# Hash attention and MLP on one core: the first two chunks run by another table of the same operations

## The chip, the cores and the metric

The kernel runs on one core of a Trainium2 chip. The metric is the device time of one execution in microseconds (us). TensorE (PE; its weight loads are shown as PEld), VectorE (DVE), ScalarE (ACT), GpSimd (POOL) and SyncE (SP) each work through a list of instructions of their own, in order, and wait for one another by semaphores.

## The reference

What is computed, cut to what matters (q, k, v are 4 batches x 8 heads x 768 tokens x 64; d_model is 512, the hidden width 2048):

```python
    q_bits = (np.einsum('bhsd,dk->bhsk', q, proj) > 0).astype(np.int64)
    k_bits = (np.einsum('bhsd,dk->bhsk', k, proj) > 0).astype(np.int64)
...
    mask = q_bucket[:, :, :, None] == k_bucket[:, :, None, :]
    scores = scale * np.matmul(q, k.transpose(0, 1, 3, 2))
    scores = np.where(mask, scores, -1000000000.0)
    scores = scores - np.max(scores, axis=-1, keepdims=True)
    attn = np.exp(scores)
    attn = attn / (np.sum(attn, axis=-1, keepdims=True) + 1e-09)
    return np.matmul(attn, v).astype(np.float32)
...
    xn = (x - mu) / np.sqrt(var + 1e-06) * g_ln
    ch = np.maximum(xn @ w_ch1, 0.0) @ w_ch2
    return (x + ch).astype(np.float32)
```

## The kernel before

**Chunks, pairs, groups.** The work is cut into 12 chunks: 4 batches x 3 stretches of 256 query tokens. A chunk's attention has 4 pairs of heads with 3 groups each, 12 units. A unit has a scores half (L513: four matmuls of 256 columns into the PSUM tile sc, then one exponential on ScalarE, L519, into ex) and a values half (L534: 16 or fewer small matmuls av <- ex, vaug). The third group of a pair ends with a quotient on VectorE (L562, L572). In batch 0 an epsilon term is added on TensorE before it (L549): with six matmuls if the pair's values have not been summed yet, with one if they have. A chunk's MLP is a norm on VectorE, eight "ups" (hp, L653) and eight "downs" (o, L675). In chunk n the attention of chunk n is interleaved with downs of chunk n-2 and ups of chunk n-1.

**Operands.** Scores are taken with 70 rows: 64 of q or k in bf16 and 6 of hash bits, side by side in the tile slots. For batch 0 each head's q and k are transposed on TensorE (tpose, L237), evacuated from PSUM to qkT (L247, L249 on VectorE, L251 on ScalarE), cast into slots in two halves, par 0 and par 1 (L196 on VectorE or GpSimd, L192 on ScalarE), hashed on TensorE (L356 for one head, L384 for a pair), compared with zero on VectorE (bits, L365, L391), and the bit rows are copied into slots (L196, L192). For the batches after it GpSimd narrows q and k (N, L270), a transposing DMA on SP's queue writes slots (L294), the odd tokens are copied to their place (L194 by DMA, or L196 on GpSimd), and the bits go through DRAM (L326, L333). The xnT of all chunks but the first is a transposing DMA on SP's queue too (L637). SP's queue also has all loads of q, k, v (L147, L182) and all outputs (L684). GpSimd issues the loads of the weights (L699, L706).

**What sets the order.** The first two chunks, half of chunk 2 and the preparation of batches 0 and 1 are written out by hand in a string, FIRST_TWO, that the function first_two runs from left to right; each engine gets its instructions in that order. The letters, with the head or half first and the engine that is to do it (V, A, G) last: T is a transpose with its evacuation (T31V: head 3, k, evacuated by VectorE; a small s or a at the end puts it into a buffer of the score or the values pool of PSUM instead of the common pool mm), C a cast (C40G: head 4, par 0, GpSimd), h and H a hash of a head or a pair, r and B bit rows, P the values of a pair, R their sums, z and Z matmuls that only keep TensorE busy, W weights, S, X, Y, U, M parts of the MLP of chunks 0 and 1, L, N, V, K, O, D the preparation of batch 1, Q squares for a check at the end. "<" is the next scores half and ">" the next values half of a list of units that the string ORDER gives. In the texts S2.1 is the scores half of unit 1 of chunk 2, V0.11 the values half of unit 11 of chunk 0. In chunks 2 to 8 a dictionary, plan, names what is prepared for the batches after: three parts of a chunk (parted by "|"), each spread over fillers.

**Buffers.** sc has 2 buffers, and transposes marked s take turns in them; av has 2, with those marked a and z; mm has 2; ex has 3; qkT has 4.

Of the kernel before, what the change touches and what calls it, by code (L numbers as in the profile page):

```python
# [28 lines left out]
def kernel(  # L29
# [753 lines left out]
    FIRST = 6  # L783
    mlp = {n: mlp_steps(*chunks[n], xs[n]) for n in range(2)}

    ORDER = "020 000 0012 0212 01 10 20 30 11 31 21 12"
    FIRST_TWO = """
z3 Z20 p T00V T01Aa C00A C01G T10As h0m T11Aa r0VVGA C10V h1m C11V < z3 r1VVVV T20A T30As < T31V T21V < P0 C30V e C31G C20V >
< >
H1 P1 >  # L790
T40As B1VVVV < T41A W0 < >
R1V < R0V C41V >
T50Aa C40G C21A T51V >
< C50V H2 < >
T60Va T61A < C51G T70V >
T71V < P3 B2VGAV >
>
C60G < C61G H3 >
< P2 C71V B3VVVV W1 >
< S0 L0 R2V b < >  # L800
R3V v0 C70G < W2 >
< >
< >
Z12 < >
< >
< S1 >
X0 N00 >
X1 < Y0A K011 < Y1V L1 >
V0 < N01 >
U0 U1 < U2 >  # L810
K001 O0 K000 >
< U3 < U4 >
< K010 U5 >
K101 D0 U6 < >
>
< U7 < Q010 Q011 K110 M >
K100 K111 >
Q001 Q000
"""

    def first_two():
# [94 lines left out]

        groups = [[int(c) for c in g] for g in ORDER.split()]
        seq = [(n, 3 * j + g) for j, n, *gs in groups for g in gs or range(3)]
# [7 lines left out]
                run(op)  # L926

    plan = {
# [264 lines left out]
```

## Time and profile before

| | us |
|---|---|
| median of 3 runs | 304.8 (304.37 to 306.12) |
| the profiled execution | 305.38 |
| its span in the trace | 303.7 |

The granted TensorE clock was full (1.00) in the profiled execution. Busy times are of the span. The start of an exponential depends on its scores, the start of values on their exponential. Times are from the span's start. A row of a timeline is start, duration, engine, line, operation, output <- input, and in brackets how long the engine was idle before and what released it; rows that follow one another are merged with a count (x3). In the view by stretches the columns are length, then busy time (with count) of PE, PEld, DVE, ACT and POOL, the granted clock, the share of the DMA engines, and GB/s. In the grouped view a row ends with busy time, mean ns of one, and idle time before with its releaser.

### The profile page before, as it was taken

The numbers are of one execution on the slowest core, as the hardware profiler recorded it, in microseconds if no ns is written. First come the engines' busy times: TensorE is split into PE (matmuls) and PEld (weight loads), VectorE is DVE, ScalarE is ACT, GpSimd is POOL, SyncE is SP. The second block draws the span as 40 slices with busy tenths as digits, with TensorE's granted clock in tenths as the row PEclk, the third lists the DMA queues.
The fourth block names the chain that finished last, engine by engine and source line by source line (L and its number), as shares of the span: only waits on it lengthen the run. The fifth ranks groups of instructions, "written<-read, shape, count | busy, mean of one in ns | idle before, by whom it ended". The sixth has DMA issues, their size and how long they took to land.

```text
span 303.7 us, 7929 instructions
## 1 busy us (share of the span) xinstructions
PE 295.2 (97%) x3285; PEld 224.7 (74%) x3309; DVE 179.8 (59%) x409; ACT 215.6 (71%) x273; POOL 91.3 (30%) x117
## 2 busy tenths in 40 slices
PE   8999899999999999999999999999999999999995
PEld 5677788578688688678678678679679678687564
DVE  1998678845659459634964954633733734646322
ACT  4899986967788778669578687879677667665020
POOL 3559490685403424500831730200300200201100
PEclk9999999999999999999999999999999999999999
DMA  6999999588296379777487274330110210200302
GB/s 197 367 311 252 260 256 185 120 192 260 42 141 194 89 214 200 161 231 246 140 142 205 19 154 113 21 96 2 35 71 2 64 42 2 69 37 3 106 3 73
DMA packets 64361, 40.40 MB, mean 133 GB/s; under 512 B 44864, under 2 KB 60224, under 8 KB 64320
## 3 DMA queue, kind: packets, MB, share of 16 engines
q1 hardware_dynamic: 61024, 35.64, 47.2%
q0 software_dynamic: 3216, 4.20, 7.8%
q8 instruction: 27, 0.44, 0.6%
q14 instruction: 14, 0.11, 0.1%
q10 hardware_dynamic: 80, 0.00, 0.0%
HBM read 27.97 MB, written 6.88 MB: 115 GB/s over the span
## 4 chain that ended last, share of the span: by engine, by line
PE 93%; DVE 2%; ACT 2%; DMA 1%; issue 1%; SPq 0%; DVEq 0%; ACTq 0%
PE hp L653 28%; PE o L675 27%; PE sc L513 20%; PE av L534 11%; PE hash L313 3%; PE tpose L237 2%; ACT ex L519 1%; DMA knat<-in_k_dram 1%; PE av L549 1%; DVE slots L196 1%; PE hash L384 1%; DVE xn L600 0%; DVE bits L365 0%; PE hash L356 0%; ACT slots L192 0%
## 5 line engine op out<-in xcount | busy, mean ns | idle before, releaser
L519 ACT ACTIVATE ex<-sc,expb 128x1024 bf16<-128x1024 f32 x144 | 159.0, 1114 | 55.5 <-PE sc L513 54.0
L653 PE MATMUL hp<-xnT,w_sb 128*128 128x256 bf16 x768 | 97.7, 272 | 0.1
L675 PE MATMUL o<-w_sb,hbuf 128*128 128x512 bf16 (+1 forms) x376 | 93.1, 370 | 1.0
L513 PE MATMUL sc<-slots 70*128 70x256 bf16 x576 | 87.0, 272 | 0.8 <-ACT ex L519 0.4
L653 PEld LDWEIGHTS <-w_sb 128*128 128x128 bf16 x768 | 72.4, 97 | 9.4 <-issue 0.5
L534 PEld LDWEIGHTS <-ex 128*128 128x128 bf16 x1152 | 53.4, 97 | 15.5 <-ACT ex L519 2.3
L513 PEld LDWEIGHTS <-slots 70*128 70x128 bf16 x576 | 52.0, 97 | 15.5 <-issue 2.7
L534 PE MATMUL av<-vaug,ex 128*128 128x65 bf16 x1152 | 58.0, 193 | 0.7 <-ACT ex L519 0.7
L132 DVE TENSOR_SCALAR hbuf<-hp 128x512 bf16<-128x512 f32 x47 | 32.4, 690 | 43.2 <-PE hp L653 42.5
L675 PEld LDWEIGHTS <-hbuf 128*128 128x128 bf16 x400 | 36.9, 97 | 26.6
L136 ACT ACTIVATE hbuf<-hp 128x512 bf16<-128x512 f32 x49 | 29.1, 595 | 17.8 <-PE hp L653 17.3
L680 DVE SCALAR_TENSOR_TENSOR x<-o,rs,x 128x512 f32<-128x512 f32 (+1 forms) x25 | 18.1, 725 | 31.9 <-PE o L675 31.7
L642 POOL TENSOR_SCALAR rs<-mv 128x2 f32<-128x2 f32 x11 | 7.1, 643 | 90.3 <-DVE mv L627 90.3
L419 POOL CAST vaug<-vnat 128x1536 bf16<-128x1536 f32 x6 | 8.8, 1465 | 45.6 <-DMA vnat<-in_v_dram 28.2
L564 DVE TENSOR_SCALAR rc<-av 128x4 f32<-128x4 f32 x36 | 5.7, 157 | 27.9 <-PE av L534 27.9
L572 DVE TENSOR_TENSOR x<-x,rc 128x256 f32<-128x256 f32 x36 | 17.6, 489 | 1.0
L628 DVE SCALAR_TENSOR_TENSOR xn<-x,mv,gbc 128x512 bf16<-128x512 f32 x22 | 17.7, 840 | 0.1
L565 DVE TENSOR_TENSOR x<-av,vsum 128x256 f32<-128x256 f32 x36 | 14.9, 415 | 0.0
L626 DVE BATCH_NORM_STATS2 stats<-x 128x6 f32<-128x512 f32 x22 | 14.1, 677 | 0.2
L218 ACT ACTIVATE qnat<-qnat 128x768 f32<-128x768 f32 x16 | 13.4, 839 | 0.0
L218 ACT ACTIVATE knat<-knat 128x768 f32<-128x768 f32 x16 | 13.4, 836 | 0.0
L428 POOL TENSOR_TENSOR vsum<-vsum,vaug 128x256 f32<-128x256 f32 x18 | 12.7, 708 | 1.1
(87 smaller groups left out, 208.8 us busy)
## 6 DMA issues: line engine op xcount, KB each, us to landing
out_dram<-x SPq DMA_DIRECT2D x23, 256.0 KB
vnat<-in_v_dram SPq DMA_DIRECT2D x7, 768.0 KB
qnat<-in_q_dram SPq DMA_DIRECT2D x11, 384.0 KB
knat<-in_k_dram SPq DMA_DIRECT2D x11, 384.0 KB
w_sb<-in_moe_w_ch_dram POOLq DMA_DIRECT2D x3, 1024.0 KB, 19.1
qnat<-in_q_dram SPq DMA_DIRECT2D x2, 768.0 KB
knat<-in_k_dram SPq DMA_DIRECT2D x2, 768.0 KB
slots<-slots SPq DMA_DIRECT2D x4, 384.0 KB
```

What stands on the lines that cost most here:

```text
L132: nc.vector.tensor_scalar_max(dst, src, 0.0)
L136: nc.scalar.activation(dst, src, AF.Relu if relu else AF.Copy)
L218: done = nc.scalar.activation(src, src, AF.Square, accum_out=sq[:, a, col : col + 1])
L513: nc.tensor.matmul(sc[:, i, :], sl[0:K1, h, 1, kj * P : (kj + 1) * P], sl[0:K1, h, 0, q0 : q0 + CT],)
L519: nc.scalar.activation(ex, sc, AF.Exp, bias=expb[:, 1:2] if b else expb[:, 0:1], scale=scale if b else scale / Q_SCALE,)
L534: nc.tensor.matmul(av[:, h - ha, qi, :], state[g][:, i, qi * P : (qi + 1) * P], va[:, h, CMAP[b][kj], :], start=((g, i, qi) == (0, 0, 0)), ...
L565: nc.vector.tensor_tensor(xv, num, vs[:, ha : ha + 2, :].unsqueeze(2).to_broadcast([P, 2, TT, D]), op=AOP.add,)
L572: nc.vector.tensor_tensor(xv, num, rc.unsqueeze(3).to_broadcast([P, 2, TT, D]), op=AOP.mult)
L628: nc.vector.scalar_tensor_tensor(xn[:, :, i, :], x[:, i, :].rearrange("p (o d) -> p o d", d=P), mv[:, i, 0:1], gbc.rearrange("p (o d) -> p ...
L653: nc.tensor.matmul(hp[:, i, :], w1_sb[:, dt, nt * P : (nt + 1) * P], st["xnT"][:, dt, :], start=(dt == 0), stop=(dt == ND - 1),)
L675: nc.tensor.matmul(o2, st["h"][:, nt, i * P : (i + 1) * P], w2_sb[:, nt, cols], start=(nt == 0), stop=(nt == NH - 1),)
L680: nc.vector.scalar_tensor_tensor(x[:, i, cols], o2, st["rs"][:, i : i + 1], x[:, i, cols], op0=AOP.mult, op1=AOP.add,)
```

## The change

Both strings are replaced by others that hold the same steps, and plan has other entries for chunks 2 and 3. Cut to what says something:

```diff
-    ORDER = "020 000 0012 0212 01 10 20 30 11 31 21 12"
+    ORDER = "000 020 0012 0212 01 10 20 30 11 31 21 12"
...
-z3 Z20 p T00V T01Aa C00A C01G T10As h0m T11Aa r0VVGA C10V h1m C11V < z3 r1VVVV T20A T30As < T31V T21V < P0 C30V e C31G C20V >
+p Z20 T00As z3 T01A T10Va h0m e C01A C00G T11Aa r0VVGA h1m < C10V P0 T20Va C11V < r1VVGV z3 T30A P1 >
...
     plan = {
-        2: "| H11 E10 W11 o10 V11 L20 | J10 N11 T11 o11 N20",
-        3: "J11 E11 T20 W20 O20 | |",
+        2: "| H11 L20 E10 W11 o10 | N11 T11 N20 O11 V11 J10 J11",
+        3: "W20 E11 | T20 | O20",
```

By ORDER the first group of chunk 0 is scored before the first of chunk 2. Of the 16 evacuations VectorE now does 8 (7 before) and ScalarE 8 (9); of the 16 casts VectorE does 6 (7), ScalarE 1 (2), GpSimd 9 (7); of head 1's bit rows GpSimd does one, and of pair 2's two (one before).

ScalarE from the first exponential on, before. ex, sc, qkT and tpose carry numbers here; qkT_237, 243, 325 and 405 are heads 2, 3, 4 and 5:

```order
L519 ACTIVATE ex_227<-sc_222,expb_67 128x1024
L251 ACTIVATE qkT_237<-tpose_238 128x384
L251 ACTIVATE qkT_243<-tpose_244 128x384
L519 ACTIVATE ex_254<-sc_249,expb_67 128x1024
L519 ACTIVATE ex_271<-sc_266,expb_67 128x1024
L519 ACTIVATE ex_292<-sc_287,expb_67 128x1024
L251 ACTIVATE qkT_325<-tpose_326 128x384
L519 ACTIVATE ex_340<-sc_335,expb_67 128x1024
L251 ACTIVATE qkT_325<-tpose_342 128x384
L519 ACTIVATE ex_354<-sc_349,expb_67 128x1024
L519 ACTIVATE ex_386<-sc_381,expb_67 128x1024
L251 ACTIVATE qkT_405<-tpose_406 128x384
```

The same place now (qkT_252, 338 and 376 are heads 3, 4 and 5):

```order
L519 ACTIVATE ex_226<-sc_221,expb_67 128x1024
L519 ACTIVATE ex_242<-sc_237,expb_67 128x1024
L251 ACTIVATE qkT_252<-tpose_253 128x384
L251 ACTIVATE qkT_252<-tpose_273 128x384
L519 ACTIVATE ex_283<-sc_278,expb_67 128x1024
L519 ACTIVATE ex_290<-sc_285,expb_67 128x1024
L519 ACTIVATE ex_328<-sc_323,expb_67 128x1024
L519 ACTIVATE ex_365<-sc_360,expb_67 128x1024
L251 ACTIVATE qkT_338<-tpose_371 128x384
L519 ACTIVATE ex_387<-sc_382,expb_67 128x1024
L251 ACTIVATE qkT_376<-tpose_408 128x384
L519 ACTIVATE ex_430<-sc_425,expb_67 128x1024
```

Two exponentials now stand side by side at the start, and four (S0.1, S0.2, S2.1, S2.2) follow the evacuations of head 3 with nothing between them, where the evacuations of head 4 stood before.

GpSimd from its first cast to the second part of the weights, before:

```order
L196 CAST slots_86<-qkT 64x2x384
L196 COPY slots_86<-bits 6x2x192
L415 CAST vaug_88<-vnat 128x12x64
L196 CAST slots_86<-qkT 64x2x384
L415 CAST vaug_88<-vnat 128x12x64
L699 DMA w_sb<-in_moe_w_ch_dram 128x4x1024 x2
L196 CAST slots_86<-qkT 64x2x384 x2
L415 CAST vaug_88<-vnat_138 128x12x64
L196 COPY slots_86<-bits 6x768
L196 CAST slots_86<-qkT 64x2x384 x2
L415 CAST vaug_88<-vnat_138 128x12x64
```

The same place now, up to the last cast but one:

```order
L415 CAST vaug_88<-vnat 128x12x64
L196 COPY slots_86<-bits 6x2x192
L415 CAST vaug_88<-vnat 128x12x64
L196 CAST slots_86<-qkT 64x2x384 x2
L699 DMA w_sb<-in_moe_w_ch_dram 128x4x1024 x2
L196 CAST slots_86<-qkT 64x2x384
L415 CAST vaug_88<-vnat_138 128x12x64
L196 CAST slots_86<-qkT 64x2x384
L415 CAST vaug_88<-vnat_138 128x12x64
L196 CAST slots_86<-qkT 64x2x384 x3
L196 COPY slots_86<-bits 6x768 x2
```

Behind the first part of the weights stand five casts, two copies of bit rows and the values of two pairs (vaug <- vnat_138) in a row, and one more cast follows.

SP's queue in chunk 2, before (slots_87 is batch 1's, bits_1184 those of its second half):

```order
L333 DMA slots_87<-bits_d 6x48x32 x3
L684 DMA out_dram<-x 128x512
L326 DMA bits_d<-bits_1184 128x384
L333 DMA slots_87<-bits_d 6x48x32
L294 DMA_TRANSPOSE slots_87<-nat_1287 128x24x128
L684 DMA out_dram<-x 128x512
L147 DMA qnat<-in_q_dram 128x2x384
L147 DMA knat<-in_k_dram 128x2x384
L147 DMA qnat<-in_q_dram 128x2x384
L147 DMA knat<-in_k_dram 128x2x384
L637 DMA_TRANSPOSE xnT<-xn 128x8x128
L333 DMA slots_87<-bits_d 6x48x32 x4
```

And now (bits_1179 are the second half's):

```order
L326 DMA bits_d<-bits_1179 128x384
L147 DMA qnat<-in_q_dram 128x2x384
L147 DMA knat<-in_k_dram 128x2x384
L147 DMA qnat<-in_q_dram 128x2x384
L147 DMA knat<-in_k_dram 128x2x384
L684 DMA out_dram<-x 128x512
L294 DMA_TRANSPOSE slots_87<-nat_1251 128x24x128
L333 DMA slots_87<-bits_d 6x48x32
L194 DMA slots_87<-slots_87 64x24x128
L333 DMA slots_87<-bits_d 6x48x32 x5
L637 DMA_TRANSPOSE xnT<-xn 128x8x128
```

The loads of batch 2 stand ahead of the transposing DMA; the odd tokens (L194) and all bit rows of the second half stand between it and the transposing DMA of the norm.

More of the change, by code (lines that the diff above doesn't have):

```diff
@@ L784 @@
     mlp = {n: mlp_steps(*chunks[n], xs[n]) for n in range(2)}
-    ORDER = "020 000 0012 0212 01 10 20 30 11 31 21 12"
+    ORDER = "000 020 0012 0212 01 10 20 30 11 31 21 12"
     FIRST_TWO = """
-z3 Z20 p T00V T01Aa C00A C01G T10As h0m T11Aa r0VVGA C10V h1m C11V < z3 r1VVVV T20A T30As < T31V T21V < P0 C30V e C31G C20V >
-< >
[L790 to L796, printed above, removed]
->
[L798 to L801, printed above, removed]
-< >
[L803 to L818, printed above, removed]
+p Z20 T00As z3 T01A T10Va h0m e C01A C00G T11Aa r0VVGA h1m < C10V P0 T20Va C11V < r1VVGV z3 T30A P1 >
+T21Vs T31Aa < < H1 C30G >
+>
+< R0V T40Vs C20G >
+W0 C31G < B1VVVV T41A T50Va < R1V P3 C41V C40G >
+T51A >
+< H2 P2 C21G < T60As C50G >
+C51G T61V B2VGAG >
+T70V < T71V C60V >
+< C71V < H3 >
+L0 C61G < W1 b >
+>
+< < B3VVVV W2 C70V >
+S0 R2V < R3V v0 >
+< >
+< Z12 >
+< K011 >
+>
+S1 < >
+X0 X1 < N00 >
+< V0 L1 Y0A >
+< Y1V N01 < >
+U0 U1 Q001 K001 >
+U2 U3 K000 < >
+U4 < K010 K101 < U5 O0 >
+< D0 U6 >
+< >
+< U7 M >
+K110 >
+< Q000 K100 Q011 >
+K111 Q010
 """
```

## The prediction

> **What bounds the kernel now.** The page first: its busy shares and the chain that ended last.
>
> ```profile
> PE 295.2 (97%) x3285; PEld 224.7 (74%) x3309; DVE 179.8 (59%) x409; ACT 215.6 (71%) x273; POOL 91.3 (30%) x117
> ...
> PE 93%; DVE 2%; ACT 2%; DMA 1%; issue 1%; SPq 0%; DVEq 0%; ACTq 0%
> ```
>
> TensorE is busy 97% of the span and makes up 93% of the chain: an average over the whole program, so the next view is the one by stretches of time.
>
> ```profile
> 10.00:20.00 10.00, 9.68 (x132) 8.18 (x133) 9.60 (x22) 9.06 (x13) 4.46 (x5) 1.00 1.06 366
> 20.00:30.00 10.00, 9.50 (x147) 7.08 (x146) 9.20 (x20) 9.54 (x11) 8.65 (x15) 1.00 1.11 252
> 30.00:40.00 10.00, 9.04 (x138) 7.42 (x136) 7.17 (x21) 9.59 (x11) 5.58 (x8) 1.00 1.13 262
> 40.00:50.00 10.00, 10.00 (x135) 8.63 (x133) 6.53 (x11) 7.05 (x9) 5.38 (x7) 1.00 1.23 222
> ```
>
> From 40 us on TensorE is full (10.00 of 10) and the other engines have room: there an edit off TensorE costs or gains nothing unless it makes TensorE wait. From 10 to 40 us TensorE is not full, ScalarE is busy 9.06 to 9.59 of 10, and VectorE 9.60 and 9.20 in the first two rows. That is the part that the table rewrites. So the question is by how much the first MLP matmul (U0 of the table) moves; whatever it moves is kept by the full TensorE behind it.
>
> The chain of waits shows how that point is reached:
>
> ```profile
> 16.72 0.68 PE av L549 x6
> ...
> 19.98 0.11 PE av L549
> ...
> 34.34 0.44 PE sc L513 x4
> 34.78 0.24 PE av L534 x8
> 35.03 0.13 PE av L549
> ...
> 39.90 1.76 PE hp L653 x16
> ```
>
> The last values group of chunk 0 ends at 35.03, then VectorE's norm follows, and the first MLP matmuls run from 39.90. Just ahead of it 0.44 us of scores of chunk 1 stand on the chain.
>
> **Part 1, ScalarE's work in the first stretch.** Two groups of ScalarE between 9.3 and 26.7 us, then rows of its timeline:
>
> ```profile
> L519 ACT ACTIVATE ex<-sc,expb 128x1024 bf16<-128x1024 f32 x11 | 12.1, 1114 | 1.5 <-PE sc L513 1.4
> L251 ACT ACTIVATE qkT<-tpose 128x384 f32<-128x384 f32 x6 | 2.8, 487 | 0.5 <-PE tpose L237 0.4
> ```
>
> ```profile
> 9.38 1.11 ACT L519 ACTIVATE ex<-sc,expb 128x1024 bf16<-128x1024 f32 x1 [0.84 <-PE sc L513]
> 10.58 0.87 ACT L251 ACTIVATE qkT<-tpose 128x384 f32<-128x384 f32 x2
> 11.34 3.21 ACT L519 ACTIVATE ex<-sc,expb 128x1024 bf16<-128x1024 f32 x3
> 14.96 0.49 ACT L251 ACTIVATE qkT<-tpose 128x384 f32<-128x384 f32 x1 [0.40 <-PE tpose L237]
> ...
> 18.27 1.11 ACT L519 ACTIVATE ex<-sc,expb 128x1024 bf16<-128x1024 f32 x1 [0.37 <-PE sc L513]
> ...
> 19.96 0.84 ACT L192 ACTIVATE slots<-qkT 64x768 bf16<-64x768 f32 x1
> 20.83 2.26 ACT L519 ACTIVATE ex<-sc,expb 128x1024 bf16<-128x1024 f32 x2
> ...
> 26.72 2.12 ACT L519 ACTIVATE ex<-sc,expb 128x1024 bf16<-128x1024 f32 x2
> ```
>
> Taken from start to start, an exponential holds ScalarE for 1.07 us (three in 3.21), an evacuation for 0.38 (two from 10.58 to 11.34), a cast for 0.87 (19.96 to 20.83). From the first exponential, 9.38, to the one at 26.72, from which they run on with hardly a pause, are 17.34 us: 11 x 1.07 + 6 x 0.38 + 2 x 0.87 = 15.8, and 1.55 of idle. After the change the same 11 exponentials stand ahead of that point, with five evacuations (heads 3, 3, 4, 5, 6) and one copy: 14.55. **Work saved: 1.25 us** (one evacuation, the cast C21). The first exponential doesn't come earlier: head 0 takes the same steps, with its evacuation and casts only swapped between engines.
>
> **Part 2, the pauses that the new order has.** These are my estimates; the first pause is filled by work that was there before.
>
> ```profile
> 8.68 0.60 PE L513 MATMUL sc<-slots 70*128 70x256 bf16 x4
> ```
>
> From a group's first score matmul to its exponential go 0.70 us (8.68 to 9.38). Scores have two PSUM buffers, and transposes marked s take a turn in them. Before, the evacuations of heads 2 and 3 filled the wait of the second exponential. Now: (a) two exponentials follow at once, then two evacuations, until 9.38 + 2 x 1.07 + 2 x 0.38 = 12.28; the next needs the rows of head 1, which VectorE finishes after two casts, an evacuation and three copies: 11.7 to 12.5, so a pause of 0 to 0.7, I take 0.4. (b) The exponential of S2.1 stands behind hash pair H1 on TensorE: 0.4. (c) T40 takes the buffer between S2.1 and S2.2, so that both use the same one: S2.2's matmuls can start only when the exponential of S2.1 has ended, and ScalarE has nothing between: 0.70 + 0.2 = 0.9. (d) S1.2 stands behind H2, which waits for T51: 0.5. Together 2.2, against 1.55 now: **+0.65**; bounds 0 (every pause covered) to 3.2 (each half as long again).
>
> The values of the first pair now come after its rows are summed, so that six epsilon matmuls (0.68 us) become one (0.11): 0.57 us less on TensorE, in a stretch where ScalarE's pauses decide. I count nothing and keep 0.57 as the lower bound.
>
> **Part 3, GpSimd and VectorE.** GpSimd gets two casts more and two bit-row copies more. VectorE loses a cast, a row copy of each size, and gains an evacuation.
>
> ```profile
> 8.44 0.82 POOL L415 CAST vaug<-vnat 128x768 bf16<-128x768 f32 x1
> 8.52 1.15 DVE L196 CAST slots<-qkT 64x768 bf16<-64x768 f32 x1
> ...
> 10.23 0.56 DVE L196 CAST slots<-qkT 64x768 bf16<-64x768 f32 x1
> ...
> 12.64 0.82 POOL L196 CAST slots<-qkT 64x768 bf16<-64x768 f32 x1 [3.38 <-DVE qkT L249]
> 13.53 1.04 POOL L415 CAST vaug<-vnat 128x768 bf16<-128x768 f32 x1
> 12.98 2.00 DVE L196 CAST slots<-qkT 64x768 bf16<-64x768 f32 x2
> 22.79 0.82 POOL L196 COPY slots<-bits 6x768 bf16<-6x768 bf16 x1 [0.38 <-DVE bits L391]
> ...
> 23.68 1.69 POOL L196 CAST slots<-qkT 64x768 bf16<-64x768 f32 x2
> ...
> 24.21 0.56 DVE L249 COPY qkT<-tpose 128x384 f32<-128x384 f32 x1
> ...
> 30.50 0.82 POOL L196 CAST slots<-qkT 64x768 bf16<-64x768 f32 x1
> ```
>
> VectorE's cast takes 0.56 us alone and 1.15 when GpSimd's cast runs from 8.44 to 9.26: it ends 0.41 after it. The two casts at 12.98 end at 14.98, 0.41 after GpSimd's cast that ends at 14.57. So a cast of VectorE waits out the GpSimd operation that it meets. Four more of 0.8 us are at most 3.3 us of waiting on VectorE. Its evacuations from PSUM are not held: the one at 24.21 takes 0.56 us under two casts of GpSimd. [...]
>
> Where it counts: the bit rows of pair 3 and the second cast of head 7. Before, GpSimd ends that cast at 31.32, and the scores of heads 6 and 7 start about then. Now VectorE does it last. With ScalarE 0.6 us ahead there (1.25 - 0.65), VectorE's chain (pair 3's hash, one quotient, four rows, the cast) ends at about 31.2, and **0.4** of the lead is lost.
>
> **Part 4, the end of the stretch.** V0.11 is moved ahead of S1.4, so that the 0.44 us of scores at 34.34 no longer stand ahead of the last values: **-0.35** on the chain into the norm. The stream transpose that now stands on VectorE before it fits in the wait for those values.
>
> **Part 5, chunks 2 and 3.** The loads of batch 2 are now issued ahead of the transposing DMA of batch 1's second half; the copy of odd tokens goes from GpSimd (2.74 us) to SP's queue.
>
> ```profile
> 64.06 3.68 SPq L294 DMA_TRANSPOSE slots<-nat  x1
> 67.84 0.52 SPq L684 DMA_DIRECT2D out_dram<-x  x1
> 78.82 1.25 SPq L637 DMA_TRANSPOSE xnT<-xn  x1
> 80.18 3.01 SPq L333 DMA_DIRECT2D slots<-bits_d  x4
> 89.83 0.72 SPq L194 DMA_DIRECT2D slots<-slots  x1
> 69.67 2.74 POOL L196 COPY slots<-slots 64x3072 bf16<-64x3072 bf16 x1 [1.83 <-DMA slots<-nat]
> 84.62 1.04 PE L653 MATMUL hp<-xnT,w_sb 128*128 128x256 bf16 x8
> ```
>
> On SP the transposing DMA comes behind the output at 67.84: it is issued by 72.0, lands 1.93 us later (67.74 to 69.67 before), then follow the odd tokens (0.72) and five bit issues (0.75 each): SP is free at 78.5, and the transposing DMA of the norm was issued at 78.82. It feeds the matmuls at 84.62; with 1.25 + 1.93 us of its own it may start as late as 81.4. Cost nothing, with 2.6 us of cover.
>
> **The sum.** -1.25 + 0.65 + 0.4 - 0.35 = -0.55 us. The profiled execution took 305.4 us (span 303.7); its changed form would take 304.8. The median of the runs is 304.8, 0.6 below, so I predict 304.3.
>
> **The rivals.** (A) Faster: the pauses are no longer than before and VectorE keeps up. Then -1.25 - 0.35 - 0.57 = -2.2 us: 302.6. For it speaks that ScalarE is the fullest engine from 20 to 40 us; against it that the new order has a place (c) where nothing can fill ScalarE. (B) Slower: **the GpSimd casts hold VectorE.** Place: VectorE from 19 to 31 us, where GpSimd now does nine operations in a row. Price: 3.3 us of waiting less 0.6 of work taken off VectorE is 2.7 on the cast of head 7; less the 0.35 of part 4 it gives +2.3: 307.1. It decides from the point where that cast ends later than about 31.3. For it: the rows of 1.15 and 2.00; against: half of VectorE's operations there read PSUM. (C) Slower: **SP's queue.** If the transposing DMA behind 1.5 MB of loads lands later than 76.9 instead of 74.0, the norm's transpose is late and TensorE waits at 84.62; five us of lateness cost 2: 306.8 with the rest cancelled. Against: 2.6 us of cover.
>
> **How the numbers follow.** A measurement tells about 0.5%, 1.5 us, from no change here. Forecast (within 1.5 us) 0.55; A 0.17; B 0.16; C 0.12. Faster by over 0.5% is A, 0.17; slower is B and C, 0.28. The range goes from A to B, 302.6 to 307.1; the likeliest case alone is 303.3 to 305.8.
>
> **What would show it.** In the profile after: the first exponential still at 9.4; ScalarE idle for about 0.9 us before the sixth exponential (S2.2); the unbroken run of exponentials from about 26.1 instead of 26.72; the first MLP matmul at 39.2 instead of 39.76; no TensorE wait at 80 to 86. I am wrong if TensorE's stretches after 40 us are no longer full, if VectorE's casts in 19 to 31 us take over 1.2 us each, or if the MLP starts later than 40 us.

## The result and the profile after

The changed kernel takes 306.44 us (median of 12 runs, 304.94 to 309.07), the kernel before 305.03 beside it (12 runs, 304.02 to 306.18). The ratio is 1.0052, with an interval from 1.003 to 1.0074: slower by 1.4 us where 0.5 less than before was forecast. Single executions reach 309, those of before stay under 306.2. Here and below, medians are over all executions, while the ratio and its interval leave out those that are over 1.5% above the fastest of their kernel and follow the means more than the medians, so the ratio is not the quotient of the two medians. The profiled execution of the changed kernel is one of its quickest (305.21 us, span 303.6); that of the kernel before (305.38) stood above its median. So the two traces show where time goes, and not how much it is at the median.

The page of the changed kernel, busy shares and the chain that ended last:

```profile
PE 294.9 (97%) x3280; PEld 223.8 (74%) x3304; DVE 176.2 (58%) x407; ACT 214.6 (71%) x271; POOL 91.6 (30%) x120
...
PE 83%; DMA 6%; POOL 4%; DVE 3%; ACT 2%; issue 1%; SPq 0%; DVEq 0%; POOLq 0%; ACTq 0%
```

TensorE has fallen from 93% to 83% of the chain, and DMA has risen from 1% to 6%: transfers now end waits that lie on the path. ScalarE's timeline of the changed kernel shows the first stretch:

```profile
9.36 2.12 ACT L519 ACTIVATE ex<-sc,expb 128x1024 bf16<-128x1024 f32 x2 [0.84 <-PE sc L513]
11.37 0.87 ACT L251 ACTIVATE qkT<-tpose 128x384 f32<-128x384 f32 x2
12.18 2.12 ACT L519 ACTIVATE ex<-sc,expb 128x1024 bf16<-128x1024 f32 x2
14.87 1.11 ACT L519 ACTIVATE ex<-sc,expb 128x1024 bf16<-128x1024 f32 x1 [0.57 <-PE sc L513]
16.73 1.12 ACT L519 ACTIVATE ex<-sc,expb 128x1024 bf16<-128x1024 f32 x1 [0.74 <-PE sc L513]
...
21.18 1.11 ACT L519 ACTIVATE ex<-sc,expb 128x1024 bf16<-128x1024 f32 x1 [0.35 <-PE sc L513]
```

The first exponential comes at 9.36 as before, and the pauses are 0 (no bracket at 12.18), 0.57, 0.74 and 0.35. TensorE's timeline has the start of the MLP, and behind it two rows that the kernel before doesn't have:

```profile
38.62 1.91 PE L653 MATMUL hp<-xnT,w_sb 128*128 128x256 bf16 x16
...
78.72 0.39 PE L513 MATMUL sc<-slots 70*128 70x256 bf16 x2 [0.37 <-DMA slots<-bits_d]
...
84.50 1.05 PE L653 MATMUL hp<-xnT,w_sb 128*128 128x256 bf16 x8 [0.32 <-DMA xnT<-xn]
```

The MLP starts 1.14 us earlier (38.62 against 39.76), but the matmuls that stood at 84.62 before now stand at 84.50. Most of the lead is lost between 70 and 90 us. The view by stretches of the changed kernel agrees (TensorE's 10 us there were 9.89 and 10.00 full before):

```profile
70.00:80.00 10.00, 9.52 (x95) 6.54 (x96) 7.31 (x15) 7.89 (x11) 4.47 (x4) 1.00 0.51 108
80.00:90.00 10.00, 9.68 (x111) 7.50 (x108) 3.81 (x8) 7.19 (x11) 1.91 (x2) 1.00 0.99 183
```

SyncE's timeline of the changed kernel tells what is late; start and duration are those of the issue:

```profile
61.25 0.43 SPq L147 DMA_DIRECT2D qnat<-in_q_dram  x1
...
62.76 0.47 SPq L147 DMA_DIRECT2D knat<-in_k_dram  x1
64.19 0.36 SPq L684 DMA_DIRECT2D out_dram<-x  x1
64.65 6.12 SPq L294 DMA_TRANSPOSE slots<-nat  x1
70.82 0.74 SPq L333 DMA_DIRECT2D slots<-bits_d  x1
74.38 0.70 SPq L194 DMA_DIRECT2D slots<-slots  x1
75.14 6.07 SPq L333 DMA_DIRECT2D slots<-bits_d  x5
81.31 1.28 SPq L637 DMA_TRANSPOSE xnT<-xn  x1
```

The four loads of batch 2 (two of their rows are left out) stand ahead of the transposing DMA. Its issue takes 6.12 us instead of 3.68, and it lands at 74.37 (in the chain, "64.65 9.72 DMA slots<-nat") instead of 69.67. The odd tokens (74.38) wait for it, and the bits of head 3 are issued behind them, at 75.14; in the kernel before they went ahead of the transposing DMA:

```profile
63.22 0.74 SPq L333 DMA_DIRECT2D slots<-bits_d  x1
```

The other four of the five bit issues, those of the second half, wait once more, until the odd tokens have landed. SyncE's waits between 60 and 90 us name it:

```profile
SPq L333 <- DMA slots<-slots: 2.2, 1, 2.2
```

So the norm's transpose is issued at 81.31 instead of 78.82.

### The profile page after: what moved, and what is told of

Its sections match the earlier page's. It is cut to its first block, busy times and chain, and to the rows that moved or that the text cites. A ratio compares the mean times of both kernels' runs of the same rounds, so it can differ in the third digit from the quotient of the medians.

```text
span 303.6 us, 7917 instructions
## 1 busy us (share of the span) xinstructions
PE 294.9 (97%) x3280; PEld 223.8 (74%) x3304; DVE 176.2 (58%) x407; ACT 214.6 (71%) x271; POOL 91.6 (30%) x120
## 4 chain that ended last, share of the span: by engine, by line
PE 83%; DMA 6%; POOL 4%; DVE 3%; ACT 2%; issue 1%; SPq 0%; DVEq 0%; POOLq 0%; ACTq 0%
PE hp L653 25%; PE o L675 23%; PE sc L513 18%; PE av L534 10%; DMA slots<-nat 3%; PE hash L313 2%; PE tpose L237 2%; ACT ex L519 1%; DMA slots<-bits_d 1%; DMA xnT<-xn 1%; DVE slots L196 1%; POOL nat L270 1%; POOL slots L196 1%; PE hash L384 1%; DMA qnat<-in_q_dram 1%
## 5 line engine op out<-in xcount | busy, mean ns | idle before, releaser
L680 DVE SCALAR_TENSOR_TENSOR x<-o,rs,x 128x512 f32<-128x512 f32 (+1 forms) x25 | 18.1, 725 | 33.1 <-PE o L675 32.9
L572 DVE TENSOR_TENSOR x<-x,rc 128x256 f32<-128x256 f32 x36 | 16.8, 467 | 1.0
L628 DVE SCALAR_TENSOR_TENSOR xn<-x,mv,gbc 128x512 bf16<-128x512 f32 x22 | 16.7, 796 | 0.1
L270 POOL CAST nat<-qnat 128x1536 bf16<-128x1536 f32 x6 | 9.2, 1530 | 17.7 <-DMA qnat<-in_q_dram 9.0
```

Source lines behind the costliest of these rows:

```text
L572: nc.vector.tensor_tensor(xv, num, rc.unsqueeze(3).to_broadcast([P, 2, TT, D]), op=AOP.mult)
L628: nc.vector.scalar_tensor_tensor(xn[:, :, i, :], x[:, i, :].rearrange("p (o d) -> p o d", d=P), mv[:, i, 0:1], gbc.rearrange("p (o d) -> p ...
L680: nc.vector.scalar_tensor_tensor(x[:, i, cols], o2, st["rs"][:, i : i + 1], x[:, i, cols], op0=AOP.mult, op1=AOP.add,)
```

## The experiments

Two theories stood at the start. **Q**: the loss is in SyncE's queue, which the new plan fills; the new strings gain. **T**: the new strings themselves cost. A third, **L**, came with the first results: the strings cost because T20Va, the transpose of head 2's q, now stands right behind S0.0 on TensorE, where its load hasn't landed yet. Each run has its own runs of the kernel before on the same chip beside it. "Behind the MLP's start" is a profiled execution's time less the start of its first hp matmul: 265.62 us for the kernel before (305.38 - 39.76), 266.59 for the changed one.

**e1: new strings, old plan.**

```diff
-        2: "| H11 L20 E10 W11 o10 | N11 T11 N20 O11 V11 J10 J11",
-        3: "W20 E11 | T20 | O20",
+        2: "| H11 E10 W11 o10 V11 L20 | J10 N11 T11 o11 N20",
+        3: "J11 E11 T20 W20 O20 | |",
```

> The new strings FIRST_TWO and ORDER with the old plan for chunks 2 and 3. Theory Q (the new strings gain 1.1 us, as the first MLP matmul at 38.62 instead of 39.76 shows, and SP's queue in chunk 2 gives back that and more): 1.1 us faster than before, 303.9 us, ratio 0.996. Theory T (the strings themselves are slower in most executions, for instance where GpSimd waits for loads of v, and the profiled one was lucky; the plan is neutral): 306.4 us, ratio 1.005.

305.72 against 304.74, ratio 1.0033 (1.0016 to 1.005). Theory Q missed here: the strings alone are not faster, they cost about 1 us. Behind the MLP's start it takes 265.61, as before. The MLP starts at 39.80. TensorE's timeline names a wait that I had not seen:

```profile
9.95 0.55 PE L237 MATMUL tpose<-identf,qnat 128*128 128x128 f32 x3 [0.98 <-DMA qnat<-in_q_dram]
```

SyncE's and GpSimd's timelines show that under the old plan, too, the new strings bring the loads of batch 2 ahead of the transposing DMA. Its issue is as long, and it lands at 77.4, 3 us later than in the full change:

```profile
62.44 1.51 SPq L333 DMA_DIRECT2D slots<-bits_d  x2
...
65.82 0.39 SPq L147 DMA_DIRECT2D qnat<-in_q_dram  x1
...
67.89 5.94 SPq L294 DMA_TRANSPOSE slots<-nat  x1
76.67 1.24 SPq L637 DMA_TRANSPOSE xnT<-xn  x1
```

```profile
77.43 2.74 POOL L196 COPY slots<-slots 64x3072 bf16<-64x3072 bf16 x1 [10.45 <-DMA slots<-nat]
```

Yet TensorE waits for nothing between 70 and 90 us: the bits of heads 2 and 3 (62.44) went ahead of it, and the norm's transpose (76.67) doesn't wait for the odd tokens. So the late transposing DMA is not the loss by itself; what stands behind it decides.

**e2: old strings, new plan** (the other half of the change).

> The old strings with the new plan. Theory Q: slower than before by what the queue costs, less than in the full change since TensorE comes to the scores that wait 1.1 us later: 305.5 to 306.5 us, ratio 1.002 to 1.005, with a wait of TensorE for slots or xnT between 77 and 86 us. Theory T: as before, 305.0 us, ratio 1.000, and no such wait.

306.32 against 304.74, ratio 1.0047 (1.0029 to 1.0065). The plan alone costs as much as the whole change. The MLP starts at 38.71, and from there it takes 266.87, 1.25 more than before; TensorE's timeline has

```profile
77.53 0.61 PE L513 MATMUL sc<-slots 70*128 70x256 bf16 x4 [0.96 <-DMA slots<-bits_d]
```

So the plan costs in chunk 2, as Q says, but not by a late transposing DMA: with the old strings it stands ahead of the loads, and its issue is short. SyncE's timeline:

```profile
61.60 3.68 SPq L294 DMA_TRANSPOSE slots<-nat  x1
...
66.44 0.44 SPq L147 DMA_DIRECT2D qnat<-in_q_dram  x1
...
69.01 0.75 SPq L194 DMA_DIRECT2D slots<-slots  x1
69.81 10.72 SPq L333 DMA_DIRECT2D slots<-bits_d  x6
```

Here the bits of heads 2 and 3 stand behind the loads and the odd tokens, and the first of these rows lands 7.68 us after its issue (in the chain, "69.81 7.68 DMA slots<-bits_d"). The two halves don't add up (1.0 + 1.6 against 1.4): an execution that comes to 77 us late waits less there (0.96 us in e2, with the MLP from 38.71; 0.29 in e5 below, from 39.30).

**e3: the full change, the odd tokens copied by GpSimd as before** (O11 becomes o11 in the plan).

> The full change, but the odd tokens of batch 1's second half are copied by GpSimd again instead of by a DMA on SP's queue; the loads of batch 2 stay ahead of the transposing DMA. Theory Q with the odd tokens as the piece that holds the queue (SP waits 3.1 us for the transposing DMA to land before it issues them, and 2.2 us behind them): the bit rows of head 3 and the norm's transpose come some 4 us earlier, TensorE has no wait at 78 and 84 us: 303.9 to 304.3 us, ratio 0.996 to 0.998. If instead the early loads are the piece: still 305.5 or more. Theory T: 306.4 us.

308.81 against 304.74, ratio 1.0111 (1.0082 to 1.014): worse, a miss. GpSimd's timeline:

```profile
75.79 1.46 POOL L270 CAST nat<-qnat 128x1536 bf16<-128x1536 f32 x1 [8.71 <-DMA slots<-nat]
77.20 1.93 POOL L270 CAST nat<-knat 128x1536 bf16<-128x1536 f32 x1
79.19 2.74 POOL L196 COPY slots<-slots 64x3072 bf16<-64x3072 bf16 x1
```

GpSimd too waits for the transposing DMA, and its copy of 2.74 us, which meets the quotient on VectorE (1.91 us instead of 0.42), comes behind two casts. In SyncE's queue the bits of the second half wait for that copy, until 81.96, and the norm's transpose stands behind them:

```profile
72.27 12.66 SPq L333 DMA_DIRECT2D slots<-bits_d  x6
85.05 1.26 SPq L637 DMA_TRANSPOSE xnT<-xn  x1
```

TensorE waits 1.91 us for xnT at 88.18 (and 1.37 us at 84.56, where the profile names no releaser). In e1, where GpSimd copies as well and the transposing DMA lands later, its copy comes ahead of the casts and the norm's transpose ahead of these bits, and TensorE doesn't wait. So the run shows the order in the queues, and not which engine should copy.

**e4: the full change, the bits of the first half ahead of the transposing DMA.**

```diff
-        2: "| H11 L20 E10 W11 o10 | N11 T11 N20 O11 V11 J10 J11",
+        2: "| H11 L20 E10 W11 o10 J10 | N11 T11 N20 O11 V11 J11",
```

> The full change, but the last two bit rows of batch 1's first half (heads 2 and 3) are issued ahead of the transposing DMA. Theory Q: the wait of TensorE for head 3's bits (0.37 us at 78.7 in the profiled execution) goes, the wait for the norm's transpose at 84.5 stays and grows, since TensorE comes to it earlier: 304.7 to 305.7 us, ratio 0.999 to 1.002. Theory T: 306.4 us.

306.6 against 304.74, ratio 1.0057 (1.0043 to 1.0072). The wait for bits is gone, and the next in the queue takes its place: the bits of the second half wait 3.1 us for the odd tokens (issued at 75.73) to land, and the norm's transpose comes behind them, at 82.73. TensorE's timeline:

```profile
85.92 1.05 PE L653 MATMUL hp<-xnT,w_sb 128*128 128x256 bf16 x8 [1.64 <-DMA xnT<-xn]
```

**e5: the full change, the loads of batch 2 behind the transposing DMA.**

```diff
-        2: "| H11 L20 E10 W11 o10 | N11 T11 N20 O11 V11 J10 J11",
+        2: "| H11 E10 W11 o10 | N11 T11 L20 N20 O11 V11 J10 J11",
```

> The full change, but the loads of batch 2 are issued behind the transposing DMA of batch 1's second half. Theory Q (SP's queue in chunk 2 costs 1.0 to 1.7 us behind the first MLP matmul): if the early loads are what makes that DMA land late, the waits for bits and for the norm's transpose go and the kernel is as the strings alone, 305.7 us, ratio 1.003; if the odd tokens on SP's queue are, it stays at 306.4 us, ratio 1.005.

305.6 against 305.0, ratio 1.0035 (1.0014 to 1.0055): about the loss of the strings alone, though the interval overlaps that of the full change. It takes 265.93 us behind the MLP's start. SyncE's timeline has the short issue again:

```profile
62.50 3.69 SPq L294 DMA_TRANSPOSE slots<-nat  x1
```

The bits of heads 2 and 3 now stand behind the loads, as in e2, and TensorE waits 0.29 us for them at 77.46; its MLP started at 39.30, later than in e2.

**g3: the full change, the four loads issued in the same place by GpSimd.**

```diff
-                fetch(nc.sync, nm, lo, hi)
+                fetch(nc.gpsimd if (b, half) == (2, 0) else nc.sync, nm, lo, hi)
```

> The full change, the four loads of batch 2 issued in the same place by GpSimd instead of SyncE. If the transposing DMA is late because it stands behind 1.5 MB in SyncE's own queue: its issue takes 3.7 us again, it lands by about 72, and the median falls to that of the change with the loads behind (305.6, 0.6 above the kernel before). If it is late because the data of the loads keeps the DMA engines busy whoever issues them: its issue still takes about 6 us, the waits at 76 to 86 us stay, and the median stays 1.2 to 1.7 above.

305.4 against 304.76, ratio 1.0016 (1.0 to 1.0032). The same data moves ahead of the transposing DMA, but in another queue, and TensorE waits for nothing between 70 and 90 us. SyncE's timeline:

```profile
64.73 4.34 SPq L294 DMA_TRANSPOSE slots<-nat  x1
...
71.04 0.70 SPq L194 DMA_DIRECT2D slots<-slots  x1
...
78.96 1.28 SPq L637 DMA_TRANSPOSE xnT<-xn  x1
```

The transposing DMA's issue takes 4.34 us against 6.12, and the odd tokens go out at 71.04 against 74.38. That points to the place in SyncE's own queue. But GpSimd issues these loads between 55.45 and 58.97, SyncE from 61.25 on, so the run doesn't part the queue from the earlier time.

**f1: e1 with T20Va moved behind S2.0.**

```diff
-< C10V P0 T20Va C11V < r1VVGV z3 T30A P1 >
+< C10V P0 C11V < r1VVGV T20Va z3 T30A P1 >
```

> The new strings with the old plan, and one step moved: the transpose of head 2's q (T20) stands behind the second scores, the casts and the bit rows of head 1, instead of ahead of them. Theory L (the new strings are slower because this transpose stands at the head of TensorE's and VectorE's queue before its load has landed: TensorE waited 1.0 us for it at 9.95 in the profiled execution of the strings alone, and head 1's rows came late): about as before or faster, 304.0 to 304.9 us, ratio 0.998 to 1.001, and a narrower spread of the executions. Theory G (the four operations more on GpSimd, and the VectorE copies that wait behind them, cost the 1.0 us): as the strings alone, 305.5 to 306.0 us, ratio 1.003.

305.08 against 305.0, ratio 1.0018 (0.9991 to 1.0044). The median is that of before, as L expects, but the interval overlaps that of e1, and two of 12 executions lie above 308. So theory G of that text, by which GpSimd's added operations cost the 1.0 us, isn't excluded by this run. The loads stand ahead of the transposing DMA here too (its issue takes 6.60 us), the MLP starts at 38.93, and TensorE waits for nothing between 70 and 90 us.

**f2: e1 with q and k of heads 2 and 3 loaded ahead of the first v; f3: the kernel before with the same loads,** its control.

```diff
-            if b == 0 and half == 0 and lo == 2:
-                t["v"] = load_values(b, half, 0, 2)
             for nm in "qk":
                 fetch(nc.sync, nm, lo, hi)
+            if b == 0 and half == 0 and lo == 2:
+                t["v"] = load_values(b, half, 0, 2)
```

> The new strings with the old plan, and the loads of q and k of heads 2 and 3 issued ahead of the first load of v (0.4 MB) instead of behind it. Theory L: q of head 2 lands about 1 us earlier, ahead of its transpose: 304.0 to 305.0 us, ratio 0.998 to 1.001. Theory G: 305.5 to 306.0 us, ratio 1.003.

> The old strings and the old plan with the same order of loads: the control. The old strings come to these transposes later (9.99 us), so theory L expects no gain: 304.6 to 305.2 us, ratio 1.000 to 1.002. If the order of loads helps any table, as much as the one before: 303.8, ratio 0.997.

f2: 307.13 against 305.0, ratio 1.0075 (1.0049 to 1.0101), a miss for L. f3: 305.22, ratio 1.0001 (0.9987 to 1.0016); its one profiled execution took 1078.72 us and is not used. In f2 the v of heads 0 and 1 came late instead (GpSimd waited 2.15 us for it), and the granted clock fell to 0.50. The view by stretches, clock third from the right:

```profile
12.00:14.00 2.00, 0.64 (x7) 0.34 (x6) 1.92 (x4) 0.49 (x1) 1.59 (x2) 1.00 1.06 383
14.00:16.00 2.00, 1.91 (x15) 0.69 (x20) 0.36 (x1) 1.59 (x2) 1.57 (x2) 0.50 1.07 378
16.00:18.00 2.00, 2.00 (x34) 1.11 (x19) 0.92 (x2) 0.64 (x1) 1.76 (x3) 0.50 1.04 339
```

This doesn't test L: the transposes no longer wait, but another load does.

**g1: the full change with both pieces undone; g2: with T20Va behind S2.0 alone.** The edits are those of f1 and e5.

> The full change with both suspected pieces undone: head 2's first transpose (T20Va) stands behind S2.0, and the loads of batch 2 stand behind the transposing DMA. Two causes (late q of heads 2 and 3, early loads): nothing else is left that costs, so the median is that of the kernel before within 0.4 us, as in the strings with only T20Va moved (305.08 against 305.00). One more cause in the plan (odd tokens and bits on the queue of SyncE): 0.5 to 1.2 us above the kernel before, with TensorE waiting for bits or for xnT between 76 and 86 us.

> The full change with T20Va behind S2.0 and the early loads kept. Early loads cost: the attention's lead reaches the MLP, and the queue takes it and more: 1.0 to 1.6 us above the kernel before, as with the old strings under the new plan (1.58), and TensorE waits for slots<-bits_d or xnT at 76 to 86 us. If the strings were the whole cause: within 0.4 us of the kernel before.

g1: 305.27 against 304.76, ratio 1.0019 (0.9994 to 1.0043). g2: 306.38 against 304.76, ratio 1.0056 (1.0035 to 1.0077). With the early loads T20's place changes nothing (1.0052 and 1.0056): TensorE waits for the bits of head 3 at 79.41 and for xnT at 85.03, as in the full change. Without them the middle is near that of before, but five of g1's 12 executions lie above 306.9, up to 310.85. The profiled one (308.85) shows, in TensorE's timeline, a wait at the branch ahead of the last 16 matmuls:

```profile
300.36 3.52 PE L675 MATMUL o<-w_sb,hbuf 128*128 128x256 bf16 x16 [2.31 <-issue]
```

g3's profile has it too (1.67 us). So a further theory, **X**: the wait at the branch is part of the loss.

**h1, h2, h3: the changed kernel, the kernel before, and g1, each without the branch (the test of the flag and the general path are left out); h4: g1 with the branch's hint set earlier.**

```diff
-    tc.mark_branch_hint_location(
...
-    ok = nc.values_load(flag[0:1, 0:1], min_val=0, max_val=1)
-    with tc.If(ok < 1, label="general") as cmp:
...
+    for _, f in downs[6:]:
+        f()
```

> The full change without the branch ahead of the last two downs (the test of the check's flag and the general path are left out). If the loss is all in the queue and the late q (theory Q and L): still 1.0 to 1.5 us above the kernel before without the branch. If the wait at the branch makes the loss: within 0.4 us of the kernel before without the branch, and no execution over 307.

> The kernel before without the branch (same work left out): the control. Its executions show no wait at the branch, so no more than 0.5 us below the kernel before by either theory, with the same small spread.

> The full change with T20Va behind S2.0 and the loads behind the transposing DMA, without the branch. If the waits at the branch make the spread of this order (304.0 to 310.9): no execution over 306.5, and a median 0.3 to 0.6 below the kernel before without the branch. If the spread comes from the first stretch (loads of q and v): single executions above 307 stay.

> The full change with T20Va behind S2.0 and the loads behind, and with the branch, its hint set some 10 us earlier. If TensorE waits there because its instructions are fetched too late: no wait in the profile at 298, no execution over 306.5, and the median 0.3 below the kernel before. If an early hint is of no use: waits and spread as in the same kernel with the late hint (304.0 to 310.9).

Beside 304.65 for the kernel before: h1 306.27, ratio 1.0049 (1.0029 to 1.0069); h2 304.46, 0.9993 (0.9978 to 1.0008); h3 305.7, 1.0028 (1.0004 to 1.0052); h4 305.08, 1.0031 (1.0003 to 1.006). X falls: without the branch the change loses 306.27 - 304.46 = 1.8 us, no less, h4 is as g1, and h3 still has an execution of 309.33. That one was profiled, and it shows what made it long. VectorE's timeline, then TensorE's, then the stretches:

```profile
36.32 0.98 DVE L275 STREAM_TRANSPOSE bt<-knat 128x768 f32<-128x768 f32 x1 [2.94 <-DMA knat<-in_k_dram]
```

```profile
39.57 0.40 PE L616 MATMUL xnTp<-ident,xn 128*128 128x128 bf16 x4 [1.89 <-DVE xn L600]
...
41.60 3.46 PE L653 MATMUL hp<-xnT,w_sb 128*128 128x256 bf16 x16
```

```profile
38.00:40.00 2.00, 0.43 (x11) 0.44 (x12) 1.93 (x6) 0.89 (x2) 0.19 (x1) 1.00 1.15 266
40.00:42.00 2.00, 2.00 (x30) 1.76 (x27) 1.39 (x4) 1.44 (x2) 1.92 (x3) 0.84 1.16 267
42.00:44.00 2.00, 2.00 (x11) 1.39 (x10) 0.47 (x1) 1.27 (x2) 2.00 (x2) 0.50 1.18 250
```

This is the stream transpose K011 of batch 1's k. The new strings put it ahead of the last quotient of chunk 0 on VectorE; before, it stood behind the norm's xn (38.33). Here its k comes at 36.3, the quotient and the norm wait behind it, TensorE idles for 1.89 us ahead of xnTp, and the granted clock is 0.84 and then 0.50: 16 hp matmuls take 3.46 us instead of 1.91.

**i1: the full change with K011 behind the norm; i2: all three pieces mended.**

```diff
-< K011 >
+< >
...
-< Y1V N01 < >
+< Y1V K011 N01 < >
```

> The full change with the stream transpose K011 behind the norm (behind Y1V) instead of ahead of the last quotient of chunk 0; early loads and T20Va as in the change. If K011's wait is a third cause, beside the other two: about 0.5 below the change (some 305.8, 0.9 above the kernel before) and no execution over 308. If the queue of SyncE alone sets the change's loss: still 1.2 to 1.6 above.

> The full change with all three pieces mended: T20Va behind S2.0, the loads of batch 2 behind the transposing DMA, K011 behind the norm. If K011's wait makes the spread of the kernel with two pieces mended (304.0 to 310.9, median 0.5 above the kernel before): no execution over 306.5, and the median 0.3 to 0.7 below the kernel before. If the spread comes from elsewhere (the loads of q and v at 9 to 19 us, the branch at the end): single executions over 307 stay, and the median is that of the kernel before or 0.5 above.

i1: 305.95 against 305.19, ratio 1.0032 (1.0011 to 1.0054). i2: 305.2 against 305.19, ratio 1.0006 (0.9988 to 1.0025). i1's median is where a third cause puts it, but two executions lie above 308 (308.1, 310.33), which was not expected. In i2 none lies above 306.65, where g1, with K011 in its new place, reached 310.85. It does not beat the kernel before, which I had expected: its MLP starts at 38.63, and TensorE's timeline then has

```profile
77.50 0.61 PE L513 MATMUL sc<-slots 70*128 70x256 bf16 x4 [1.02 <-DMA slots<-bits_d]
```

The bits of heads 2 and 3 still stand behind the loads and the odd tokens on SyncE; in the kernel before they are issued ahead of the transposing DMA (61.41 and 63.22). SyncE's timeline of i2:

```profile
68.60 11.21 SPq L333 DMA_DIRECT2D slots<-bits_d  x6
```

The first of these six lands 8.86 us after its issue. An early MLP therefore gains nothing. The loads behind and these bits ahead, both at once, was not tried, nor were the strings with both T20Va and K011 moved under the old plan.

**g4: f1 with T40 in the common pool** instead of the score pool.

> The new strings with T20Va behind S2.0 (as before under the old plan) and T40 in the common pool instead of the score pool. If T40's turn in the score buffers costs the pause before S2.2's exponential (0.75 us in the strings' profile): that pause falls to 0.2 or less, the first MLP matmul comes about 0.5 earlier (38.4), and the median is 0.5 below that of the strings alone, 0.4 below the kernel before. If the following steps wait for something else (head 3's evacuations, the common pool), the pause only moves and the median stays at that of the kernel before.

306.45 against 304.76, ratio 1.0047 (1.0022 to 1.0072), where 0.4 below was expected. The pause ahead of S2.2 fell only from 0.75 to 0.46, and in the profiled execution K011 waited 2.21 us for its k, so that the MLP started at 40.49. The run doesn't tell what T40's buffer is worth.

## Why the prediction was wrong, step by step

| profiled execution | first hp matmul | from there to the end |
|---|---|---|
| before | 39.76 | 265.62 |
| e1 (strings alone) | 39.80 | 265.61 |
| after | 38.62 | 266.59 |
| e2 (plan alone) | 38.71 | 266.87 |
| g2 (T20 moved) | 39.09 | 266.66 |
| e5 (loads behind) | 39.30 | 265.93 |
| i2 (all three mended) | 38.63 | 266.74 |
| f1 (old plan, T20 moved) | 38.93 | 265.91 |

**Part 1 (work of ScalarE, -1.25)** held: from the first exponential to the one that stood at 26.72 before go 16.21 us after (9.36 to 25.57), against 17.34; less the pauses below that is 14.55, as forecast.

**Part 2 (pauses, +0.65)** named the right places; the sizes in the profiled execution are 0, 0.57, 0.74 and 0.35 = 1.66, against 0.4, 0.4, 0.9 and 0.5 = 2.2. Pause (a) is the one that varies. From the first exponential to the third go 2.82 us after, 4.46 in e1 (13.53 - 9.07). I derived it from VectorE's steps and didn't ask when the q of head 2 lands: its transpose now stands ahead of them.

**Part 3 (GpSimd and VectorE, +0.4)**: of the casts into slots that VectorE starts from 19 to 31 us one takes 1.01 us, while GpSimd copies (23.90 to 25.82), the others 0.55 and 0.56, and the last one (29.88, 0.55) ends at 30.4, not 31.2. VectorE's timeline:

```profile
24.13 1.01 DVE L196 CAST slots<-qkT 64x768 bf16<-64x768 f32 x1
```

Rival B didn't come. That a meeting can be dear was right, but here it cost little: this cast, and one of 0.83 us at 18.89, while GpSimd casts (18.49 to 19.31). Not every meeting held VectorE: the cast at 25.71 took 0.56 though GpSimd's, which started behind it (25.89 to 26.96), met it, and the one at 29.88 took 0.55 beside GpSimd's small copies (L711, 28.60 to 31.17). In e3 a quotient of 0.42 us, beside GpSimd's copy of 2.74 us, took 1.91.

**Part 4 (last values, -0.35)** rests on the sentence that the stream transpose "fits in the wait for those values". In the profiled execution it does: it starts at 32.64, takes 0.98, and the quotient follows at 34.07 without loss. There it would stop to fit if its k landed later than 34.07 - 0.98 = 33.1. (The last group of values before ended at 35.16; the 35.03 of the prediction is the start of its last row, and the sum doesn't use it.) In five other profiles with the new strings it waited for its k until later than that (33.27 in f1, 33.82 in g2, 33.84 in g3, 35.22 in g4 and 36.32 in h3).

**The sum of parts 1 to 4 (-0.55)** failed at the median: e1 is 1.0 slower. The change of the work was right. What it put at nothing are two waits for loads (T20's q, K011's k), now early in the queues of TensorE and VectorE, and a load's landing varies from profile to profile (in the six in which K011 waited for its k, it started between 32.64 and 36.32). That these two make the whole 1.0 is not shown. The row that the sum started from hid this: 39.76 is late for the kernel before. Its median, 305.03, less the 265.62 behind gives a start of 39.4, and e2 and h2, with the old strings, start at 38.71 and 38.13.

**Part 5 ("Cost nothing, with 2.6 us of cover") is the other step that failed.** It took SyncE's queue as a sum of issues: the landing at 74.0, then 0.72 and five times 0.75, so free at 78.5. The landing came at 74.37, and that is luck of two opposite errors: the transposing DMA started 3.7 us earlier than assumed (64.65 instead of 68.4), its issue lasted 6.12 instead of 3.68, and it landed 3.6 us after that instead of 1.93. What the sum left out is the wait for the odd tokens to land, 2.2 us ahead of the last four bit issues: the queue was free at 81.2, and the norm's transpose was issued at 81.31, just inside the limit of 81.4. But that limit is for a TensorE without a lead; this one came to the matmuls at 84.18 and waited 0.32 us. And the prediction followed only the norm's transpose: the bits of head 3, which TensorE wanted at 78.35 (78.72 less the wait of 0.37), were issued behind the odd tokens and landed 3.53 us later (in the chain, "75.14 3.53 DMA slots<-bits_d"). The sign that it named, stretches after 40 us that are no longer full, came.

Rival C named the place. Its price of 2 is above the 1.0 to 1.25 us that the profiles put on the plan behind the MLP's start (after, g2, e2; e2's median says 1.6), and its point of decision, a landing later than 76.9, was wrong both ways: at 74.37 TensorE waited in the full change, at 77.4 it didn't in e1. That its 306.8 is near the measured 306.44 is luck, since it counts nothing for the strings.

What is shown: each half alone costs, the strings by e1 and the plan by e2, both with an interval above 1. In the profiles of the old plan (before, e1, f1, h2) TensorE waits for no bits and no xnT between 70 and 90 us (f2 and g4 have a wait of 0.29 and 0.25 us there without a named releaser), whether the loads stand ahead of the transposing DMA (e1, f1) or behind it; under the new plan it does in after, e2, e3, e4, e5, g2, h1, h4, i1 and i2, and not in g1, g3 and h3. So the place of the bit rows, and with them of the norm's transpose, behind the odd tokens and the loads is what costs. With the loads behind the transposing DMA only the length of its issue goes: e5 lost 0.3 us behind the MLP's start, i2, which came earlier, 1.1. How much of the median the loads' place makes is open (e5's interval overlaps that of the change). The waits for T20's q and K011's k are shown in single profiles (0.98 and up to 2.94 us); at the median each comes to about half a microsecond (e1 to f1, g1 to i2) with intervals that overlap, so their sizes stay open. With all three mended the loss is gone (1.0006); what remains for a gain is, not tried, the bits' place in the queue.

## What to carry to other kernels

Ahead of moving an instruction earlier, look up when its load lands, in several executions: VectorE stood 2.94 us at K011 in h3 with the quotient and the norm queued behind it, and 0.35 us in the profile of the changed kernel, so one profile may be the lucky one. In a queue that issues transfers, count the waits as well as the issues: in the changed kernel the last four bit issues stood 2.2 us until the odd tokens had landed, with the norm's transpose queued behind them, so what the full engine needs next goes ahead of such a wait, and ahead of bulk loads. And compare the halves of a change with the median and the profile's start of the full stretch; a lead there is worth only what the next late transfer lets through (i2's MLP started 1.13 us earlier, and TensorE then waited 1.02 us for bits).

## What the runs showed of the hardware beyond that

- The same transposing DMA was issued in 3.64 to 3.69 us with the 1.5 MB of loads behind it on SyncE (before, e2, e5, i2), in 5.84 to 7.03 with the loads ahead of it there (after, e1, e4, f1, g2, h1), in 4.34 with the loads issued by GpSimd, some 5 us earlier (g3).
- A small transfer behind the loads was late too: a bit row landed 7.68 us (e2) and 8.86 us (i2) after its issue with the loads and the odd tokens ahead of it, 3.53 in the changed kernel.
- After some waits of TensorE the granted clock fell, after others it didn't. In h3 a wait of 1.89 us was followed by a granted clock of 0.84 and 0.50 in the next two stretches of 2 us; in g1 a wait of 2.31 us by 16 matmuls in 3.52 us. But in g3 one of 1.67 us left them at 1.91, and in e3 one of 1.91 us, as long as h3's, was followed by eight hp matmuls in 1.05 us (e2 has 1.04 for them without a wait). So in these runs the length of the wait alone doesn't decide, and what does was not shown.
- At the branch ahead of the last 16 matmuls TensorE waited 1.67 us (g3) and 2.31 us (g1), with no releaser named in the profile, and not at all in the other profiles; without the branch the kernel before measures the same (0.9993).
